# A second level of seven products for both sequence matrices, with the products of the first level in another order

## The chip, the cores and the metric

The kernel runs on one core of one Trainium2 chip. The metric is the device time of one execution in microseconds; lower is better.

## The reference

The input is x, 2048 tokens by 640 features. One branch is a Fourier mixing layer, real part only, with given cosine and sine matrices; the other is a dense layer, Mish, and a second dense layer. A gate per token mixes them.

```python
a = einsum("bsd,ed->bse", x, dft_hid_re)       # 640 x 640
b = einsum("bsd,ed->bse", x, dft_hid_im)
y = einsum("ts,bse->bte", dft_seq_re, a) - einsum("ts,bse->bte", dft_seq_im, b)   # 2048 x 2048
h = einsum("bsd,df->bsf", x, w1) + b1          # F = 1728
m = einsum("bsf,fd->bsd", h * tanh(softplus(h)), w2)
g = sigmoid((x * gate_w).sum(-1, keepdims=True))
out = g * y + (1 - g) * m
```

Everything is fp32. The kernel multiplies the sequence matrices onto x first and the hidden matrices after that.

## The kernel before

**One product.** A product of two fp32 blocks is three matmuls (`mm3`): each operand is split into a high and a low fp32r part, and high x high, high x low and low x high are summed in PSUM. A matmul has 128 x 128 weights and 512 moving columns, a whole PSUM bank. For a moving operand (`operand`) ScalarE copies the high part and VectorE subtracts it for the low part; weights are cut the same way (`split`).

**Seven for eight.** The large products are written as a scheme of seven block products in place of eight (Winograd's form). A `Problem` takes two token tiles of 512 columns (`t1`, `t2`), two halves of the contraction (k and k + `kh`) and four of the five 128-column weight groups; the fifth group is multiplied plainly. A `Stage` makes the weight sums: `top` loads three weight columns, `low` makes the sums t1 to t4 and loads the lower half (`XB`: fifth, b21, b22). The stages are `seq` (kh = 8, weights from x, moving tiles from the cosine and sine matrices), `hid` (kh = 5) and `fin` (kh = 6, weights from w2).

A `Problem` has three parts. `first` multiplies a11 b11. `second` loads a11, a21 and a22 for each k and makes three products: a22 with t4, s2 with t2, s1 with t1. `third` loads a12, and a11, a21, a22 again except for the last `HOLD` k, whose sums stay in SBUF, and makes a12 with b21 ("12"), s3 with t3, s4 with b22. The sums between are `tt`, a VectorE tensor_tensor. After each product the banks are combined with further additions.

**The second level.** `Halves` takes a12 b21 of two problems together (token tiles 0 and 2) and makes it with seven products again, with sums of its own of weights (`top`) and of moving tiles. `UNITS = (1,)` says that this is done for problem q=1 and its partner q=3, the sine matrix; q=0 and q=2, the cosine matrix, make "12" plainly in `third`. The same form is used in the last stage.

**Order.** The sequence part runs second(0), third(0), second(1), third(1), the unit, second(2), third(2), second(3), third(3). Then come the hidden problems, the first dense layer and the last stage. The program is first a graph of operations (`Graph`); matmuls keep their written order, and a planner (`Graph.run`) places the operations of ScalarE, VectorE and the two DMA issuers (SP for loads, POOL for stores) by modelled costs and wanted times (`want`, `by`, `since`), and gives out tiles from pools. The pools are 8 PSUM banks, 10 operand pairs `r`, 18 fp32 tiles `f` of 512 columns, 6 fp32 tiles `x` of 640 and 26 weight pairs `w`. A pool that nobody asks for any more passes its tiles to another (`heir`).

**Beside it.** Sixteen gate sums (L1211) are spread over 60 to 210 us by their wanted times. In the last stage the weight sums are made ahead through DRAM (`make`, from `MADE`), and `rest` multiplies the last rows of w2, five blocks for a token tile.

## Time and profile before

| | |
|---|---|
| median of 3 runs | 852.66 us (852.25 to 852.85) |
| profiled execution | 852.38 us, its span 850.6 us |
| granted TensorE clock | 0.999 of full |
| TensorE (PE) busy | 845.2 us, 99%, 3715 instructions |
| weight loads (PEld) | 697.2 us, 82% |
| VectorE (DVE) | 748.1 us, 88%, 1358 instructions |
| ScalarE (ACT) | 525.7 us, 62%, 977 instructions |
| HBM | 182.39 MB read, 55.66 MB written, 280 GB/s |

Times are of one profiled execution, counted from the span's start. A busy share is an average over all stages. Lines such as L369 are those of the helpers: L369 is every product's matmul, L333 is `tt`, L342 is `copy`, L363 and L364 are `operand`, L355 is `split` on VectorE, L324 a store and L1211 a gate sum. The program's names stand without buffer numbers: `f<-ps` is a copy from a PSUM bank into an f tile. The duration of an instruction on VectorE overlaps the start of the next.

### The profile page before, as it was taken

Reading aid. Unit: us, or ns where it says so; the run is one execution under the profiler, and the core shown is the slowest. Engines: PE = TensorE matmul, PEld = TensorE weight load, DVE = VectorE, ACT = ScalarE, POOL = GpSimd, SP = SyncE. Lnnn points to the kernel's source line nnn. Section 1 sums busy time; section 2 is a strip of 40 time slices with the busy share of each in tenths; the row PEclk is TensorE's granted clock in tenths of the full one; section 3 lists DMA queues with packets and bytes.
Section 4 is the critical chain, followed back from the end, with each engine's and each line's share of the span. In section 5 each row is a group of like instructions: output and inputs, shape, how many; then the busy total and the mean of one; then the engine's idle time right before and its main releaser. Section 6 shows DMA issues by size and latency. Waiting matters only on the chain.

```text
span 850.6 us, 12496 instructions
## 1 busy us (share of the span) xinstructions
PE 845.2 (99%) x3715; PEld 697.2 (82%) x3715; DVE 748.1 (88%) x1358; ACT 525.7 (62%) x977; POOL 115.3 (14%) x210
## 2 busy tenths in 40 slices
PE   9999999999999999999999999999999999999998
PEld 7888888888888788888888888888888888888886
DVE  7977889977789988887999999999696889999987
ACT  6967765537456646454678773666578877544623
POOL 0122110002001111040012102003431110002100
PEclk9999999999999999999999999999999999999999
DMA  9898695768567897999999875858999799849974
GB/s 332 319 357 283 191 326 156 258 228 298 173 215 248 291 383 250 329 363 384 329 332 326 263 262 195 297 186 304 383 326 336 244 321 334 264 124 269 317 267 173
DMA packets 119603, 238.90 MB, mean 281 GB/s; under 512 B 15200, under 2 KB 23136, under 8 KB 119536
## 3 DMA queue, kind: packets, MB, share of 16 engines
q1 hardware_dynamic: 102512, 184.95, 64.6%
q0 software_dynamic: 16880, 53.03, 17.7%
q8 instruction: 29, 0.48, 0.2%
q14 instruction: 38, 0.31, 0.1%
q10 hardware_dynamic: 144, 0.13, 0.0%
HBM read 182.39 MB, written 55.66 MB: 280 GB/s over the span
## 4 chain that ended last, share of the span: by engine, by line
PE 94%; DVE 3%; DMA 2%; issue 1%; ACT 0%; DVEq 0%; ACTq 0%
PE ps L369 93%; DVE f L333 2%; DMA f<-in_xn_dram 1%; PE ps L1189 0%; DMA f<-in_c_im_dram 0%; DVE r2l L364 0%; DVE r1l L364 0%; DVE ps L333 0%; DVE r8l L364 0%; DVE r3l L364 0%; DVE r4l L364 0%; DVE r9l L364 0%; DVE r7l L364 0%; DVE r6l L364 0%; ACT r2h L363 0%
## 5 line engine op out<-in xcount | busy, mean ns | idle before, releaser
L333 DVE TENSOR_TENSOR f<-f,f 128x512 f32<-128x512 f32 (+1 forms) x371 | 238.5, 662 | 17.3 <-DMA f<-late 5.9
L342 ACT ACTIVATE f<-ps 128x512 f32<-128x512 f32 x177 | 102.6, 595 | 41.3 <-PE ps L369 36.2
L333 DVE TENSOR_TENSOR f<-ps,f 128x512 f32<-128x512 f32 x100 | 65.7, 685 | 18.9 <-PE ps L369 16.8
L342 ACT ACTIVATE ps<-f 128x512 f32<-128x512 f32 x77 | 45.5, 597 | 9.2 <-DVE f L333 8.3
L324 POOL DMA_DIRECT2D act<-f x52 | 28.3, 544 | 134.9 <-ACT f L815 110.1
L324 POOL DMA_DIRECT2D u<-f x40 | 21.6, 543 | 175.9 <-DVE f L333 161.4
L815 ACT ACTIVATE f<-f,b1s 128x512 f32<-128x512 f32 x36 | 26.1, 724 | 29.7 <-DVE f L333 29.7
L363 ACT ACTIVATE r5h<-f 128x512 fp32r<-128x512 f32 x42 | 26.4, 630 | 26.0 <-DVE f L333 15.7
L363 ACT ACTIVATE r7h<-f 128x512 fp32r<-128x512 f32 x42 | 26.4, 629 | 20.0 <-PE ps L369 10.1
L363 ACT ACTIVATE r1h<-f 128x512 fp32r<-128x512 f32 x41 | 25.8, 628 | 18.9 <-DVE f L333 7.8
L363 ACT ACTIVATE r3h<-f 128x512 fp32r<-128x512 f32 x42 | 26.4, 627 | 17.2 <-PE ps L369 10.5
L333 DVE TENSOR_TENSOR x<-x,x 128x256 f32<-128x256 f32 (+3 forms) x80 | 35.6, 458 | 1.0 <-DMA x<-in_xn_dram 0.9
L363 ACT ACTIVATE r4h<-f 128x512 fp32r<-128x512 f32 x41 | 25.8, 630 | 17.0 <-PE ps L369 13.9
L363 ACT ACTIVATE r2h<-f 128x512 fp32r<-128x512 f32 x37 | 23.3, 629 | 20.9 <-DVE f L333 10.2
L363 ACT ACTIVATE r9h<-f 128x512 fp32r<-128x512 f32 x40 | 25.2, 629 | 17.0 <-PE ps L369 14.6
L363 ACT ACTIVATE r6h<-f 128x512 fp32r<-128x512 f32 x38 | 23.9, 629 | 18.9 <-PE ps L369 12.2
L363 ACT ACTIVATE r8h<-f 128x512 fp32r<-128x512 f32 x38 | 23.9, 628 | 15.9 <-PE ps L369 9.7
L363 ACT ACTIVATE r0h<-f 128x512 fp32r<-128x512 f32 x36 | 22.6, 628 | 16.4 <-PE ps L369 7.4
L364 DVE TENSOR_TENSOR r9l<-f,r9h 128x512 fp32r<-128x512 f32 x40 | 27.4, 685 | 4.2 <-ACT r9h L363 4.1
L364 DVE TENSOR_TENSOR r3l<-f,r3h 128x512 fp32r<-128x512 f32 x42 | 28.8, 685 | 2.3 <-ACT r3h L363 2.3
L364 DVE TENSOR_TENSOR r5l<-f,r5h 128x512 fp32r<-128x512 f32 x42 | 28.8, 686 | 2.2 <-ACT r5h L363 1.8
L364 DVE TENSOR_TENSOR r7l<-f,r7h 128x512 fp32r<-128x512 f32 x42 | 28.8, 686 | 2.0 <-ACT r7h L363 2.0
(2371 smaller groups left out, 2745.4 us busy)
## 6 DMA issues: line engine op xcount, KB each, us to landing
f<-in_c_im_dram SPq DMA_DIRECT2D x126, 256.0 KB, 4.5
f<-in_c_re_dram SPq DMA_DIRECT2D x110, 256.0 KB, 4.8
f<-act SPq DMA_DIRECT2D x89, 256.0 KB, 5.2
f<-u SPq DMA_DIRECT2D x62, 256.0 KB, 4.8
act<-f POOLq DMA_DIRECT2D x52, 256.0 KB, 4.9
f<-in_xt_dram SPq DMA_DIRECT2D x42, 256.0 KB, 4.9
u<-f POOLq DMA_DIRECT2D x40, 256.0 KB, 4.1
x<-in_xn_dram SPq DMA_DIRECT2D x24, 320.0 KB, 3.8
```

Of the source, the lines that this page charges most:

```text
L324: dma(queue, lambda: ISSUE[queue].dma_start(d.t, v.t[:rows]), whole(v), whole(d), rows * N * 4)
L333: dve(lambda: nc.vector.tensor_tensor(o.t[rows, x], a.t[rows, y], b.t[rows, z], op=op), whole(a, b), whole(o), n)
L342: act(lambda: nc.scalar.activation(o.t, a.t, AF.Copy, scale=scale), whole(a), whole(o))
L363: act(lambda: nc.scalar.activation(r.t[0][:, :N], src.t[:, :N], AF.Copy), whole(src), [(r, 0)])
L364: dve(lambda: nc.vector.tensor_tensor(r.t[1][:, :N], src.t[:, :N], f32(r.t[0][:, :N]), op=OP.subtract), whole(src) + [(r, 0)], [(r, 1)])
L369: G.add("PE", lambda: nc.tensor.matmul(bank.t, w.t[wn][:, k * P:k * P + P], x.t[xn_][:, :N], start, stop, skip_group_check=True), [(w, (k, ...
L815: act(lambda: nc.scalar.activation(o.t[rows], src.t[rows], AF.Mish, **more), whole(src, table) + whole(b1s) * bias, whole(o), more=0.1)
```

## The change

`UNITS` becomes (0, 1): a12 b21 of the cosine matrix is made by a second unit of seven, which stands after third(0); q=0 and q=2 no longer make "12". The sums of the unit's weights are made once, so they move from the unit of q=1 to that of q=0.

In `second` the products are now s3 with t3, s2 with t2, s1 with t1; a22 with t4 ("22") moves to `third`. s2 is kept from `second` to `third`, in SBUF in the sequence and hidden stages (`HOLD_S2`), through DRAM in the last one, so `third` loads a12 and a22 only (and s2 in the last stage). The banks' combination changes with it: the s3 product (`c22`) is added to bank `a` and to the result on VectorE, and `rest` of t2 moves from the start of `second` to its end.

The lower weights `XB` are loaded and split by `late` in `third` instead of by `low`; the loads of `low` in the sequence stage wait for 70 us. In the unit the fourth product's bank is now the copy `c1` and the sum with `u2` is made at the end. f tiles may be borrowed from the x pool (`lender`). `MADE` starts at 560 us instead of 590, and the planner's DMA rate is 364 in place of 370 KB per us.

```diff
-RATE = 370e3
+RATE = 364e3
-MADE = 590.0, 6.0
+MADE = 560.0, 6.0
+LEND = 0.0
+LOWS = {8: 70.0, 5: 0.0}
-HOLD = {8: 3, 5: 3, 6: 0, 7: 0}
-UNITS = (1,)
+HOLD = {8: 0, 5: 0, 6: 0, 7: 0}
+HOLD_S2 = {8: 8, 5: 5, 6: 0, 7: 0}
+UNITS = (0, 1)
+LATE = (8, 5)
...
+        def spare(p):
+            q = p.lender
+            return max(0, len(q.free) - bisect_left(q.asks, (now + LEND,))) if q else 0
...
+    FS.lender = X
...
+        def late(self, k):
+
+            if k in self.XB:
+                return
+            g = load(X, self.row(k + self.kh), cols=D)
+            if self.neg:
+                copy(g, g, -1.0)
+            self.XB[k] = Val(W)
+            split(self.XB[k], 0, g, 0, D)
...
-            for p, k in in_turn(kh, *[("22", "s2", "s1")] * 3):
-                if p == "22":
+            for p, k in in_turn(kh, *[("s3", "s2", "s1")] * 3):
+                if p == "s3":
                     low(k)
                     a22, a21, a11 = self.moving(t2, k + kh), self.moving(t2, k), self.moving(t1, k)
+                    tt(a21, a21, a11, OP.subtract)
...
-                        tt(a21, a21, a22, OP.add)
-                        tt(a11, a21, a11, OP.subtract)
-                        own.update({("22", k): a22, ("s1", k): a21, ("s2", k): a11})
+                        s2 = a22
+                        tt(s2, a22, a21, OP.add)
+                    if k >= kh - HOLD_S2[kh + self.last]:
+                        self.held["s2", k] = s2
+                    else:
+                        store(self.kept[k], s2)
+                    tt(a11, s2, a11, OP.add)
+                    own.update({("s3", k): a21, ("s1", k): a11, ("s2", k): s2})
...
                 elif p == "s2":
-                    u2 = [self.add_y(v, y, 2 + j, t1) for j, v in enumerate(self.a)]
+                    u2 = [to_sbuf(v) for v in self.a]
+                    for v, o in zip(self.a, c22):
+                        tt(v, v, o, OP.add)
...
+            for v, u, o in zip(b, u2, c22):
+                tt(v, v, u, OP.add)
+                tt(o, v, o, OP.add)
...
                     a12 = self.moving(t1, k + kh)
-                    if k in self.held:
-                        a21, a22 = self.held.pop(k)
-                    else:
-                        a11, a21, a22 = self.moving(t1, k), self.moving(t2, k), self.moving(t2, k + kh)
-                        tt(a21, a21, a11, OP.subtract)
-                        tt(a22, a22, a21, OP.add)
-                    tt(a22, a12, a22, OP.subtract)
-                    own.update({("12", k): a12, ("s3", k): a21, ("s4", k): a22})
+                    s2 = self.held.pop(("s2", k)) if ("s2", k) in self.held else load_of(FS, self.kept[k])
+                    tt(s2, a12, s2, OP.subtract)
+                    own.update({("12", k): a12, ("s4", k): s2})
+                if p != "s4":
+                    st.late(k)
...
-                elif p == "s3":
-                    product(self.a, st.blocks("t3", k), x, False, end)
-                    product([self.d2], st.blocks("five", k), x, False, end)
+                elif p == "22":
+                    product(self.a, st.blocks("t4", k), x, False, end)
+                    product([self.d2], st.blocks("low5", k), x, False, end)
...
                 (c, c1), d1 = self.part.c, self.part.d1
-                for o, v, q in ((c, p, c), (d1, d, d1), (u2, u2, c1)):
+                for o, v, q in ((c, p, c), (d1, d, d1), (u2, b, u2)):
                     tt(o, v, q, OP.add)
-            tt(b, b, u2, OP.add)
+                b = c1
+            if self.into:
+                tt(b, b, u2, OP.add)
...
-                for v, j in ((c, 0), (d1, 4), (b, 1)):
+                tt(u2, b, u2, OP.add)
+                self.give(1, t1, u2)
+                for v, j in ((c, 0), (d1, 4)):
                     self.done(v, j, t1)
```

## Rows read from the trace of the kernel before

**Rows 1.** The page, busy time of each engine, us, share of the span, instructions.

```profile
PE 845.2 (99%) x3715; PEld 697.2 (82%) x3715; DVE 748.1 (88%) x1358; ACT 525.7 (62%) x977; POOL 115.3 (14%) x210
```

**Rows 2.** Waits of TensorE: engine, line, releaser; us in total, times, longest.

```profile
PE ps L1189 <- PEq L1361: 0.8, 1, 0.8
PE ps L369 <- DVE ps L333: 0.5, 1, 0.5
```

**Rows 3.** The chain that ended last: start us, us, what.

```profile
285.30 561.33 PE ps L369 x2475
```

**Rows 4.** Windows by stage: length, each engine's busy us (x instructions), clock, DMA.

```profile
70.00:118.00 48.00, 48.00 (x213) 39.77 (x212) 36.85 (x77) 34.52 (x69) 9.26 (x18) 1.00 0.78 265
118.00:156.80 38.80, 38.80 (x173) 32.10 (x172) 37.89 (x79) 26.00 (x53) 1.08 (x2) 1.00 0.66 211
156.80:200.30 43.50, 43.50 (x193) 36.03 (x192) 35.77 (x63) 19.49 (x33) 4.20 (x8) 1.00 0.69 237
200.30:238.40 38.10, 38.10 (x170) 31.53 (x169) 29.36 (x48) 21.25 (x36) 1.23 (x3) 1.00 0.69 231
238.40:265.60 27.20, 27.20 (x122) 22.52 (x121) 25.73 (x52) 12.96 (x25) 1.63 (x3) 1.00 0.61 199
265.60:296.00 30.40, 29.89 (x132) 24.45 (x131) 29.99 (x56) 21.28 (x40) 3.82 (x8) 1.00 0.93 302
```

**Rows 5.** Timeline at the one wait: start us, us, engine, line, operation.

```profile
283.36 0.68 DVE L333 TENSOR_TENSOR f<-ps,f 128x512 f32<-128x512 f32 x1
...
283.96 0.68 DVE L333 TENSOR_TENSOR f<-f,f 128x512 f32<-128x512 f32 x1
...
284.56 0.69 DVE L333 TENSOR_TENSOR ps<-ps,f 128x512 f32<-128x512 f32 x1
...
285.30 0.50 PE L369 MATMUL ps<-r2h,w9h 128*128 128x512 f32 x1 [0.51 <-DVE ps L333]
```

**Rows 6.** Timeline of VectorE, narrower and wider operations.

```profile
60.58 0.76 DVE L333 TENSOR_TENSOR x<-x,x 128x256 f32<-128x256 f32 x2
...
66.89 0.82 DVE L355 TENSOR_TENSOR w11l<-x,w11h 128x640 fp32r<-128x640 f32 x1
67.63 0.68 DVE L333 TENSOR_TENSOR f<-ps,f 128x512 f32<-128x512 f32 x1
...
72.83 0.28 DVE L355 TENSOR_TENSOR w10l<-x,w10h 128x128 fp32r<-128x128 f32 x1
73.03 0.28 DVE L355 TENSOR_TENSOR w12l<-x,w12h 128x128 fp32r<-128x128 f32 x1
```

**Rows 7.** Windows by stage, weight splits of VectorE (L355) alone.

```profile
118.00:156.80 38.80, 9.56 (x20) 1.00 0.66 211
```

**Rows 8.** Timeline at the end of second(0), TensorE, then ScalarE.

```profile
153.17 0.39 PE L369 MATMUL ps<-r5h,w8l 128*128 128x512 f32 x1
...
153.85 0.39 PE L369 MATMUL ps<-r5h,w21l 128*128 128x512 f32 x1
...
156.79 0.39 PE L369 MATMUL ps<-r7h,w13h 128*128 128x512 f32 x1
...
153.61 0.58 ACT L342 ACTIVATE f<-ps 128x512 f32<-128x512 f32 x1
...
154.61 0.59 ACT L342 ACTIVATE f<-ps 128x512 f32<-128x512 f32 x1
```

**Rows 9.** Windows: the last stage's two second parts, then the busiest slice.

```profile
700.00:736.00 36.00, 36.00 (x160) 29.81 (x159) 35.26 (x66) 25.24 (x51) 1.61 (x3) 1.00 0.95 324
...
783.00:818.00 35.00, 35.00 (x156) 29.00 (x155) 31.09 (x52) 16.32 (x29) 4.25 (x6) 1.00 1.00 326
...
380.00:400.00 20.00, 20.00 (x90) 16.57 (x89) 13.86 (x23) 7.91 (x14) 2.69 (x5) 1.00 1.04 383
```

More of the change, by code (lines that the diff above doesn't have):

```diff
@@ L3 @@
 from contextlib import ExitStack
+from itertools import count
 import concourse.bass as bass
@@ L176, in granted, with take @@
             return True
+        def spare(p):
+            q = p.lender
+            return max(0, len(q.free) - bisect_left(q.asks, (now + LEND,))) if q else 0
+        def take(v):
+            p = v.pool
+            if p.free:
+                return p.free.pop(0)
+            q = p.lender
+            t = q.free.pop(0)
+            v.home = q, t
+            return q.part(t)
         def bequeath(p):
@@ L206, in run @@
                             v.pool.soon.remove(v.ask)
-                        v.t = v.pool.free.pop(0)
+                        v.t = take(v)
                         bequeath(v.pool)
@@ L434, in low @@
                 f, t = (load_of(X, v) for v in self.made[k])
-                g = load(X, self.row(k + self.kh), cols=D)
             else:
-                f, g = load(X, self.row(k)[:, P:]), load(X, self.row(k + self.kh), cols=D)
+                apart = self.kh in LATE
+                since = LOWS[self.kh]
+                f = load(X, self.row(k)[:, P:], since=since)
+                g = load(X, self.row(k + self.kh)[:, P * apart:], cols=D - P * apart, since=since)
                 if self.neg:
-                    copy(g, g, -1.0)
+                    n = D - P * apart
+                    act(lambda: nc.scalar.activation(g.t[:, :n], g.t[:, :n], AF.Copy, scale=-1.0), whole(g), whole(g), n)
                 t = Val(X)
-                self.sums(f, g, t, P)
+                self.sums(f, g, t, P - P * apart)
             self.top(k)
@@ L444, in low @@
                 self.T2[k // KD] = Val(W)
[L445 removed]
+            c = self.XT13[k] = Val(W)
             split(self.XA[k], 3, t, 2 * P, 2 * P)
@@ L449, in low @@
             split(c, 0, f)
-            split(b, 0, g, 0, D)
+            if self.kh not in LATE and k not in self.made:
+                self.XB[k] = Val(W)
+                split(self.XB[k], 0, g, 0, D)
     def in_turn(kh, begin, between, end, n=2):
@@ L455, in in_turn @@
         return order + [(p, k) for p in end for k in range(kh - n, kh)]
+    serial = count()
     class Problem:
@@ L464, in __init__ @@
             self.apart, self.bare = apart, bare
-            self.held = {}
+            self.held, self.kept = {}, [Val(t=dr.tile([P, N], F32, name=f"s2_{next(serial)}")) for k in range(st.kh)]
         def first(self, top):
@@ L531, in second @@
                     for j, xj in fifth:
-                        product([self.d2], st.blocks("low5", j), xj, False, j == kh - 1)
+                        product([self.d2], st.blocks("five", j), xj, False, j == kh - 1)
                 elif p == "s2":
@@ L538, in second @@
                     continue
-                if p == "22":
-                    self.p4 = [self.gated(v, j) if y else to_sbuf(v) for j, v in enumerate(p4)]
+                if p == "s3":
+                    c22 = [to_sbuf(v) for v in p7]
                     if y:
@@ L543, in second, with gated @@
                             tt(v, v, y(j, t1), OP.add)
[L544 to L561 removed]
+                elif p == "s2":
+                    u2 = [to_sbuf(v) for v in self.a]
+                    for v, o in zip(self.a, c22):
+                        tt(v, v, o, OP.add)
+            if self.rest:
+                e = [bank(), bank()]
+                self.rest(t2, self.a + e + [self.d2], (0, 1, 2, 3, 4), (0, 1, 4))
+            for v, u, o in zip(b, u2, c22):
+                tt(v, v, u, OP.add)
+                tt(o, v, o, OP.add)
+            if y:
+                for j, v in enumerate(b):
+                    tt(v, v, y(2 + j, t1), OP.add)
+            if self.rest:
+                for v, o in zip(e, c22):
+                    tt(o, v, o, OP.add)
+            if not self.bare:
+                self.c = [copy(bank(), v) for v in self.p1]
+            if self.aside and not self.bare:
+                if y:
+                    tt(self.d, self.d, y(4, t1), OP.add)
+                self.d1 = copy(bank(), self.d)
+            for j, o in enumerate(c22):
+                if y:
+                    tt(o, o, self.q(t2), OP.mult)
+                    tt(o, o, y(2 + j, t2), OP.add)
+                    self.finish(2 + j, t2, o)
+                else:
+                    self.give(2 + j, t2, o)
             self.b = b
[L564 to L565 removed]
+        def gated(self, b, d):
+            f = Val(FS)
             tt(f, b, self.q(self.t2), OP.mult)
@@ L619, in third @@
                     continue
[L620 to L634 removed]
+                if p == "22":
+                    for j, v in ((0, self.a[0]), (1, self.a[1]), (4, self.d2)):
+                        if self.y:
+                            self.finish(j, t2, self.gated(v, j))
+                        else:
+                            self.done(v, j, t2)
                 elif p == "12":
@@ L1288, in fnet_mish_gate @@
                           lambda d, t: load_of(FS, later.aside[min(d, 2)]), later.finish)
-            unit.done = sq[q].done
+            unit.done, unit.give = sq[q].done, sq[q].give
             for _ in unit.steps():
@@ L1320, in fnet_mish_gate @@
                   lambda d, t, v: store(extra[min(d, 2)], v))
-    unit.done = ou[0].done
+    unit.done, unit.give = ou[0].done, ou[0].give
     for _ in unit.steps():
```

81 lines of the change are left out of this document (18 added, 63 removed).

## The prediction, made before the result was known

> **What bounds the kernel now.** I read the page's busy shares first, then TensorE's waits, the chain that ended last, and the windows by stage. TensorE is busy 99% of the span with 3715 instructions [rows 1]: eight warm-up matmuls and 3707 of work, which is exactly what counting the calls of `mm` in the code gives. After its start it waited for another engine once in the whole program, 0.5 us, for a VectorE addition into PSUM [rows 2]. So nearly nothing can be gained by ending waits; the time is the number of matmuls times their pace. The pace is read from the long unbroken piece of the chain that ended last: 2475 matmuls in 561.33 us [rows 3], 0.2268 us each.
>
> The second thing to see is how close VectorE comes. The stretches of [rows 4] are the stages of the sequence part, from the matmul counts at that pace: second(0) from 118 to 156.8 us, third(0) to 200.3, second(1) to 238.4, third(1) to 265.6, the unit of seven to 296. VectorE is busy 37.89 of 38.80 us in second(0) and 29.99 of 30.40 in the unit; between them it has slack. The one wait sits in that unit: at 283.36, 283.96 and 284.56 three additions follow each other, and the matmul at 285.30 had waited 0.51 us for the last, the addition into bank `b` [rows 5].
>
> The Trainium skill (Perfetto Trace Analysis, "Identifying the Most-Contended Engine") says that a matmul's busy share is a poor measure of TensorE, that the weight loads' share should be used, and plain occupancy for the others. By it TensorE stands at 82%, VectorE at 88% [rows 1], VectorE would be the engine to relieve, and matmuls taken away would give nothing. The trace disagrees over the whole, since the matmuls keep one pace with one wait [rows 2, 3], and agrees in the two full stretches [rows 4].
>
> **Removed matmuls.** Problem q=0 and its partner q=2 each lose the plain "12" part: 8 k x 3 blocks x 3 matmuls = 72, together 144. The second `Halves` unit has 4 k x 11 blocks x 3 = 132. The other products are renamed and reordered, and `rest` keeps its five blocks, so 12 fewer matmuls, 3703 in all: 12 x 0.2268 = **-2.72 us**. That this is not done is excluded by the count.
>
> **The one wait.** In the unit, `tt(b, b, u2)` was the sixth addition in a row and the one waited for [rows 5]. After the change `b` is the bank `c1`, filled long before, and the sum with `u2` is made at the unit's end. So **-0.51 us**, and the new unit doesn't bring its like. Lower end of the gain: 0, if the first of the remaining additions (banks `c`, `d1`) becomes the late one.
>
> **VectorE's work.** Pitch from start to start: 0.60 us for 512 columns [rows 5], 0.74 for 640, 0.20 for 128, and a pair of 256 in 0.76, so 0.34 [rows 6]. Kept s2 saves one sum for each k that was not held: 5 in each of four sequence problems, 2 in each of two hidden, 6 in each of two last ones, 36, and the last problem some 2 more. The plain "12" of q=0 and q=2 loses 16 operands (one VectorE subtraction each). The new unit adds 28 operands, 16 sums and 9 closing additions, 53. The whole is about -1 instruction: no change in the total. What counts is where they fall. In the stretch second(0), third(0), new unit:
> - before, second(0) and third(0) took 37.89 + 35.77 = 73.66 us [rows 4];
> - less 5 sums and 8 operands, 13 x 0.60 = -7.8;
> - plus 53 x 0.60 = 31.8, plus the unit's tops, which move from the later unit to this one: 16 sums of 128 columns and 8 splits of 256, 3.2 + 2.7 = 5.9;
> - plus four splits of 640 that `late` moves in from before 118 us, 2.9.
>
> That is 106.5 us. TensorE needs 420 matmuls x 0.2268 = 95.3 us there. The excess is 11.2 us. What can go ahead: in second(0) there were 20 weight splits [rows 7], five for each `low`, so four of eight `low` were still unsplit at 118 us. Without their XB they cost up to 4 sums x 0.34 + 0.33 + 0.20 + 0.20 + 0.60 = 2.7 each, 10.7 for four, and VectorE was idle 48.00 - 36.85 = 11.15 us from 70 to 118 us [rows 4]. XB no longer takes eight weight pairs at that point, so pairs for the early `low` are there. So the stretch is just full: excess between 0.5 (all four ahead) and 11.2 us (none). Gate sums and the operands of coming products can move by a few us either way. I take **+1.0 us**, two waits of the size seen in [rows 2]; bounds 0 and 11.2. I lean to the low end because second(0) alone and the unit alone ran at 98% and 99% for 0.5 us of waiting. The following stretch (second(1), third(1), old unit) gets easier: 85.1 us of VectorE in 95.7 before, without the tops and with fewer operands' sums about 76.
>
> **New waits on TensorE's path.** `a` is now added to (`c22`) on VectorE before the next stage writes it. In the trace the last two matmuls into `a` start at 153.17 and 153.85, ScalarE reads the banks at 153.61 and 154.61, and the next stage starts at 156.79 [rows 8]. One addition after the second copy (155.20 + 0.69) ends at 155.9; the second bank is wanted at 157.5. So 0.9 to 1.6 us of cover, one or two queue places on VectorE; if VectorE is further behind, "22" waits, and then s4. There are eight such places; cost 0 to 8 x 0.6 = 4.8, taken as 0 outside the full stretch. The other end sums leave with what they replace: six additions per sequence problem before and after.
>
> **Transfers.** Sequence: 28 loads of 256 KB fewer, 16 + 3 more for the unit and 8 second loads for XB: even. Hidden: -2, +5. Last stage: 12 loads become 12 stores, moved from third to second on POOL's queue. In the first of these, XB's six loads leave the same stretch (0.95 share, 324 GB/s). In the second nothing leaves: 326 GB/s at full share [rows 9], plus 6 x 0.262 MB over 35 us = 45, 371 GB/s. The busiest slice ran 383 GB/s [rows 9] without TensorE waiting [rows 2], so I take 0; upper end 1.57 MB / 383 GB/s = 4.1 us. Weights of the last stage are made 30 us earlier, away from the denser part. Borrowed x tiles only let work start earlier; POOL's stores wait for no one but the reload, over 10 us later.
>
> **Sum.** -2.72 - 0.51 + 1.0 = -2.2. The profiled execution took 852.38 us (span 850.6 and 1.8 around it), 0.3 below the median 852.66 of the runs, within their 0.6 spread. From the median: **850.4 us**.
>
> **Rivals.**
> - *VectorE sets the pace* where it is full, and TensorE gives back what it saves: half of the excess, or three to five small waits. For: two stretches of [rows 4]. Against: one wait in the whole trace. VectorE's count is unchanged, so the time is, about 852.4 us. (By the rule of the Trainium skill above it would be so everywhere.)
> - *The excess is not met.* Place: the new unit after third(0). If the four `low` stay behind 118 us (eight held s2 tiles of eighteen f tiles leave less room to work ahead), TensorE waits up to 11.2 us: 852.7 - 3.2 + 11.2 = 860.7 us. It is slower than before once more than 3.2 of the 11 us are not moved, and by over 0.2% from 4.9. Against: before, with XB in the way, half of the `low` had been moved.
> - *The last stage's stores* delay its loads: 852.7 - 3.2 + 4.1 = 853.5, place 780 to 815 us. Against: [rows 9].
>
> **Chances.** The forecast 0.58, with a range of its own from 849.1 (no new wait, and 0.3 for the spread) to 850.9. VectorE sets the pace 0.22. Excess not met 0.13. Stores 0.07, split over the bound. A measurement tells some 0.2%, 1.7 us, from no change. So faster 0.58, same 0.25, slower 0.17. Range: 849.1 to 854.2, which leaves out the unmet excess and little else.
>
> **What would show it.** Right: 3703 TensorE instructions; no wait for the `b` addition; total waits of TensorE on VectorE under 1.5 us; fewer of the `low` splits after 118 us; chain still TensorE over 90%. Wrong: VectorE full from 140 to 215 us with TensorE waiting for `r` tiles or PSUM sums in the first unit, waits before each "22", or for loads near 800 us.

## The result and the profile after

The changed kernel takes 855.91 us (median of 16 runs, 853.99 to 862.55) where the kernel before takes 852.76 (16 runs beside them, 851.95 to 853.77). The ratio is 1.0043 with an interval of 1.0031 to 1.0054: 0.43% slower, and outside the predicted range. Four executions that were 10% to several times longer than the others of their kernel (one of e4, one of e16, two of the kernel before) stand in no median, spread or ratio here. The profiled execution took 855.2 us, its span 853.0 at a granted clock of 1.000; against the profile of the kernel before that is 2.4 us more of span and 0.4 more around it.

Line numbers have moved by 19 to 32: a matmul is now L388, `tt` L352, `copy` L361, `operand` L382 and L383, `split` L373 and L374, a load L333, a store L343, a gate sum L1243. The page, busy time of each engine (answers [rows 1]):

```profile
PE 843.6 (99%) x3703; PEld 695.2 (82%) x3703; DVE 746.2 (87%) x1357; ACT 533.2 (63%) x982; POOL 121.4 (14%) x222
```

The 12 matmuls are gone and VectorE has one instruction fewer, as counted. The waits of TensorE (answers [rows 2]; engine, line, releaser; us in total, times, longest):

```profile
PE ps L388 <- ACT f L361: 3.7, 2, 2.3
PE ps L1221 <- PEq L1393: 0.8, 1, 0.8
PE ps L388 <- ACT ps L361: 0.6, 1, 0.6
PE ps L388 <- DVE r0h L380: 0.2, 1, 0.2
```

The wait for the addition into `b` has gone too. In its place stand two waits for a copy from a bank into an f tile (the row's third number is the longer, 2.3 us; the other is 1.4), one of 0.6 us for a copy into a bank, and a small one at the start. The chain that ended last shows where (answers [rows 3]; start us, us, what):

```profile
147.13 4.17 DMA x<-in_xn_dram
...
171.07 6.54 DMA x<-in_xn_dram
...
178.30 0.83 DVE x L1243 x2
...
186.72 0.54 POOL u L343
...
187.50 4.69 DMA u<-f
...
192.29 0.61 ACT f L361
...
192.94 21.41 PE ps L388 x93
...
283.07 6.02 DMA u<-f
...
289.19 0.61 ACT f L361
...
289.84 274.79 PE ps L388 x1211
...
575.08 6.38 DMA y<-f
...
588.16 0.59 ACT ps L361
...
588.80 260.11 PE ps L388 x1145
```

Before, one piece of 2475 matmuls ran to the end from 285.30. Now TensorE is stopped at 190, at 288 and at 588 us. The first two are in the two units: a store of an f tile to DRAM (`u<-f`) takes 4.69 and 6.02 us to land, ScalarE's copy wants that tile, and the next matmul wants the bank that the copy empties. Behind the first of these stores the chain leads through VectorE's queue to two loads of 320 KB: a second load of XB at 147.13, and at 171.07 the load of a gate sum, which takes 6.54 us to land (the sum itself, L1243, starts at 178.30). The profile infers who released whom, so this is a hint and not yet a proof. The timeline of the first (start us, us, engine, line, operation):

```profile
190.26 0.39 PE L388 MATMUL ps<-r9h,w4l 128*128 128x512 f32 x1
...
192.29 0.60 ACT L361 ACTIVATE f<-ps 128x512 f32<-128x512 f32 x1 [1.79 <-DMA u<-f]
...
192.94 0.50 PE L388 MATMUL ps<-r5h,w4h 128*128 128x512 f32 x1 [2.30 <-ACT f L361]
```

The windows by stage, in the bounds that the stages now have (answers [rows 4]: second(0), third(0), the new unit; then 148 to 176 us by itself; the length, the busy us of TensorE, weight loads, VectorE, ScalarE and GpSimd, clock, DMA share, GB/s):

```profile
118.00:156.80 38.80, 38.80 (x173) 32.15 (x172) 37.08 (x75) 23.51 (x45) 1.20 (x3) 1.00 0.74 246
156.80:185.00 28.20, 28.20 (x126) 23.37 (x125) 27.19 (x55) 15.87 (x31) 2.47 (x5) 1.00 0.77 282
185.00:216.00 31.00, 28.70 (x127) 23.40 (x127) 30.24 (x60) 22.21 (x41) 1.88 (x4) 1.00 0.86 282
...
148.00:176.00 28.00, 28.00 (x126) 23.16 (x125) 27.32 (x50) 16.53 (x29) 1.11 (x2) 1.00 1.00 365
```

The last line against the same stretch of the kernel before:

```profile
148.00:176.00 28.00, 28.00 (x125) 23.20 (x124) 26.44 (x50) 15.21 (x29) 0.00 (x0) 1.00 0.81 270
```

VectorE is busy 94.5 of the 98 us from 118 to 216, as foreseen. What was not foreseen is the DMA: full for 28 us, 365 GB/s where it was 270. Loads land later there. The loads of the cosine matrix issued from 148 to 176 us, with the median us to landing last; after, then before:

```profile
f<-in_c_re_dram SPq DMA_DIRECT2D x16, 256.0 KB, 5.8
...
f<-in_c_re_dram SPq DMA_DIRECT2D x19, 256.0 KB, 3.9
```

ScalarE and VectorE wait for loads in this part. Their waits on transfers from 118 to 216 us, after, the longest:

```profile
ACT r5h L382 <- DMA f<-in_c_re_dram: 2.6, 1, 2.6
ACT w8h L373 <- DMA x<-in_xn_dram: 1.8, 1, 1.8
ACT f L361 <- DMA u<-f: 1.8, 1, 1.8
ACT r9h L382 <- DMA f<-in_c_re_dram: 1.8, 1, 1.8
ACT w19h L373 <- DMA x<-in_xn_dram: 1.4, 1, 1.4
```

The whole list sums to 13.5 us; the same list of the kernel before has two groups and 4.4 us. No row of the list is a gate sum that waits for its own load; it is the other loads that come late. In 148 to 176 us eight loads of `x<-in_xn_dram`, 320 KB each, are issued where there were three: the second loads of XB, by `late`, and the gate's loads meet there, and the unit's loads are beside them.

The account by starts of matmuls: -2.72 for the 12 matmuls and -0.76 for the `b` wait (0.51, and 0.25 more until the next matmuls are at pace again); +4.27 for three waits and +0.75 for their restarts; +0.3 at the start. That is +1.8 of the 2.2 us by which the last output is written later.

### The profile page after: what moved, and what is told of

It reads as the page before. It is cut to its first block, busy times and chain, and to the rows that moved or that the text cites. A ratio compares the mean times of both kernels' runs of the same rounds, so it can differ in the third digit from the quotient of the medians.

```text
span 853.0 us, 12456 instructions
## 1 busy us (share of the span) xinstructions
PE 843.6 (99%) x3703; PEld 695.2 (82%) x3703; DVE 746.2 (87%) x1357; ACT 533.2 (63%) x982; POOL 121.4 (14%) x222
## 4 chain that ended last, share of the span: by engine, by line
PE 77%; issue 10%; DMA 5%; DVE 5%; POOL 1%; ACT 1%; SPq 0%; POOLq 0%; ACTq 0%; DVEq 0%
PE ps L388 77%; DVE f L352 1%; DMA u<-f 1%; DMA x<-in_xn_dram 1%; DMA y<-f 1%; DMA f<-in_c_im_dram 1%; POOL u L343 1%; DMA f<-in_c_re_dram 1%; DVE x L1243 0%; DMA act<-f 0%; DMA f<-in_w_dram 0%; ACT f L361 0%; DVE ps L352 0%; DVE r6l L383 0%; DVE x L352 0%
## 5 line engine op out<-in xcount | busy, mean ns | idle before, releaser
L352 DVE TENSOR_TENSOR f<-f,f 128x512 f32<-128x512 f32 (+2 forms) x321 | 205.5, 657 | 9.0 <-ACT f L847 2.1
L361 ACT ACTIVATE f<-ps 128x512 f32<-128x512 f32 x150 | 87.1, 595 | 42.3 <-PE ps L388 27.9
L352 DVE TENSOR_TENSOR f<-ps,f 128x512 f32<-128x512 f32 x102 | 68.1, 686 | 25.1 <-PE ps L388 17.1
L343 POOL DMA_DIRECT2D act<-f x50 | 27.1, 542 | 111.3 <-ACT f L847 91.3
L382 ACT ACTIVATE r1h<-f 128x512 fp32r<-128x512 f32 x39 | 24.5, 629 | 27.8 <-DVE f L352 14.9
L361 ACT ACTIVATE ps<-f 128x512 f32<-128x512 f32 x65 | 37.9, 592 | 5.7 <-DVE f L352 2.8
L343 POOL DMA_DIRECT2D u<-f x33 | 17.8, 542 | 161.3 <-DVE f L352 112.0
L352 DVE TENSOR_TENSOR x<-x,x 128x256 f32<-128x256 f32 (+3 forms) x77 | 33.5, 449 | 8.1 <-DMA x<-in_xn_dram 4.6
L382 ACT ACTIVATE r7h<-f 128x512 fp32r<-128x512 f32 x41 | 25.8, 630 | 20.2 <-PE ps L388 11.7
L382 ACT ACTIVATE r5h<-f 128x512 fp32r<-128x512 f32 x37 | 23.4, 631 | 22.9 <-DVE f L352 11.2
L382 ACT ACTIVATE r6h<-f 128x512 fp32r<-128x512 f32 x43 | 27.2, 632 | 16.3 <-PE ps L388 11.9
L382 ACT ACTIVATE r4h<-f 128x512 fp32r<-128x512 f32 x39 | 24.6, 630 | 17.9 <-PE ps L388 10.2
L382 ACT ACTIVATE r3h<-f 128x512 fp32r<-128x512 f32 x42 | 26.4, 629 | 14.9 <-PE ps L388 12.0
L383 DVE TENSOR_TENSOR r7l<-f,r7h 128x512 fp32r<-128x512 f32 x41 | 28.1, 686 | 7.8 <-ACT r7h L382 7.7
L382 ACT ACTIVATE r2h<-f 128x512 fp32r<-128x512 f32 x40 | 25.2, 631 | 14.8 <-DVE f L352 7.1
L382 ACT ACTIVATE r0h<-f 128x512 fp32r<-128x512 f32 x40 | 25.2, 629 | 12.5 <-PE ps L388 6.7
L383 DVE TENSOR_TENSOR r6l<-f,r6h 128x512 fp32r<-128x512 f32 x43 | 29.5, 685 | 3.6 <-ACT r6h L382 3.6
L383 DVE TENSOR_TENSOR r3l<-f,r3h 128x512 fp32r<-128x512 f32 x42 | 28.8, 685 | 4.3 <-ACT r3h L382 4.3
L382 ACT ACTIVATE r8h<-f 128x512 fp32r<-128x512 f32 x39 | 24.6, 630 | 10.3 <-PE ps L388 5.3
L383 DVE TENSOR_TENSOR r2l<-f,r2h 128x512 fp32r<-128x512 f32 x40 | 27.4, 686 | 4.0 <-ACT r2h L382 4.0
L382 ACT ACTIVATE r9h<-f 128x512 fp32r<-128x512 f32 x34 | 21.4, 628 | 15.2 <-PE ps L388 6.3
```

The source lines that it names most:

```text
L343: dma(queue, lambda: ISSUE[queue].dma_start(d.t, v.t[:rows]), whole(v), whole(d), rows * N * 4)
L352: dve(lambda: nc.vector.tensor_tensor(o.t[rows, x], a.t[rows, y], b.t[rows, z], op=op), whole(a, b), whole(o), n)
L361: act(lambda: nc.scalar.activation(o.t, a.t, AF.Copy, scale=scale), whole(a), whole(o))
L382: act(lambda: nc.scalar.activation(r.t[0][:, :N], src.t[:, :N], AF.Copy), whole(src), [(r, 0)])
L383: dve(lambda: nc.vector.tensor_tensor(r.t[1][:, :N], src.t[:, :N], f32(r.t[0][:, :N]), op=OP.subtract), whole(src) + [(r, 0)], [(r, 1)])
```

## The experiments

The first theory was one of tiles: f tiles are scarce, the planner believes in faster stores than there are, so copies run into tiles still being stored. The rivals were VectorE's load (the gate sums fall into its full stretch), the new order by itself, and transfers that are late. All edits are to the changed kernel unless said otherwise. Each result is the median with lowest and highest, then the ratio to the kernel before with its interval.

**e1: the planner is told that stores land later.**

```diff
-        op = G.add(queue, emit, r, w, DELAY + size / RATE, ...)
+        late = 1.2 if queue == "POOL" else 0.0
+        op = G.add(queue, emit, r, w, DELAY + late + size / RATE, ...)
...
```

> Edit: the planner is told that a transfer issued by POOL lands 1.2 us later than it assumed (about 4.1 us instead of 2.9 for 256 KB); nothing of the computation changes. Tile theory: TensorE's two waits in the units (2.3 and 1.4 us, each plus some 0.25 us of restart) come from a ScalarE copy whose only free f tile was still being stored to u. With the true landing time those copies get tiles that are free, both waits go, the time falls to about 850 us (849.5 to 851.5) and its spread narrows to that of the kernel before. VectorE theory: the copies are late because VectorE is full from second(0) to the unit; planning the stores otherwise leaves the waits, 854 to 857 us. Transfer theory: the queues are denser than before and the waits only move to loads, 853 to 857 us.

859.88 us (856.22 to 862.68), 1.0074 (1.0054 to 1.0095). Both waits for stores went, and a longer one came before them, at the first "22". The timeline of e1, VectorE and then TensorE (L354 is `tt`, L376 `split` and L390 the matmul in this kernel):

```profile
151.43 0.69 DVE L354 TENSOR_TENSOR f<-f,f 128x512 f32<-128x512 f32 x1 [1.25 <-DMA f<-in_c_re_dram]
...
156.60 0.83 DVE L376 TENSOR_TENSOR w23l<-x,w23h 128x640 fp32r<-128x640 f32 x1
...
159.15 1.89 DVE L354 TENSOR_TENSOR ps<-ps,f 128x512 f32<-128x512 f32 x3
...
159.90 0.50 PE L390 MATMUL ps<-r0h,w5h 128*128 128x512 f32 x1 [3.23 <-DVE ps L354]
```

VectorE waits 1.25 us for a load, does three weight splits of 640 columns behind it, and reaches the addition into bank `a` three microseconds late. So f tiles under store were the place of the waits in the changed kernel; with those gone the lateness shows up at another place.

**e2: fewer s2 held**, which leaves more f tiles free and costs loads.

```diff
-HOLD_S2 = {8: 8, 5: 5, 6: 0, 7: 0}
+HOLD_S2 = {8: 2, 5: 5, 6: 0, 7: 0}
```

> Edit: in the sequence stage only two of the eight s2 of a problem are held in f tiles, six go through DRAM (24 stores and 24 loads of 256 KB more). Tile theory: six of eighteen f tiles are given back between second and third, so no copy meets a tile that is being stored; waits in the units gone, about 850 us (849.5 to 852). VectorE theory: VectorE's work is the same, the waits stay, 854 to 857 us. Transfer theory: 48 transfers more in the sequence stage make it worse than the changed kernel, over 857 us.

860.95 (858.8 to 863.31), 1.0085 (1.0067 to 1.0104). Waits of 2.6 us at the "22" and 4.8 in the units; the waits on transfers of the two engines rose to 18.1 us. More free tiles with more loads is worse, as the transfer theory had it.

**e3: no gate sums.** Each sum becomes a copy of one column, the loads stay; the gate isn't computed.

```diff
-                x.t, x.t, 1.0, wide.t, op0=OP.mult, op1=OP.mult, accum_out=gcol.t[:, k:k + 1]),
+            dve(lambda k=k, x=x: nc.vector.tensor_copy(gcol.t[:, k:k + 1], x.t[:, :1]),
```

> Edit: the sixteen gate sums (L1243, 0.82 us each) are replaced by one-column copies, so the gate is not computed; their loads stay. It takes about 12 us of VectorE's work out of 50 to 205 us. VectorE theory: the excess of second(0), third(0) and the unit is gone, the wait in the first unit goes, and about 851 to 852.5 us are measured (the wait in the second unit, behind the gate sums, may stay). Tile theory: the waits for tiles under store stay, at least the second one, 853.5 to 857 us.

856.24 (854.76 to 858.75), 1.0038 (1.0025 to 1.0051). The windows of e3 from 118 to 216 us:

```profile
118.00:216.00 98.00, 96.28 (x424) 79.16 (x423) 90.80 (x181) 63.95 (x119) 6.00 (x11) 1.00 0.79 269
```

VectorE falls from 94.51 to 90.80 of the 98 us, and TensorE still stands there for 1.7 us. The waits of VectorE and ScalarE on transfers are 7.8 us, 3.4 of them of the one-column copies for their own loads. Nothing is won.

**e4: the new order without the new unit.**

```diff
-UNITS = (0, 1)
+UNITS = (1,)
```

> Edit: all of the change except the second unit: UNITS stays (1,), so q=0 and q=2 make 12 plainly, with 3707 matmuls of work. It tells what the new order, the kept s2, the late XB and the lent tiles do by themselves. Tile theory: the eight held s2 and the stores are there too, so waits of the same kind can appear in the one unit: 852 to 856 us. VectorE theory: without the second unit the stretch is not full, so no new waits: 852 to 853 us, as before.

857.05 (855.47 to 857.48), 1.0039 (1.0028 to 1.0051), longer than either expectation. The stretch from 118 to 216 us is free of TensorE waits; the DMA share in 148 to 176 is 0.81. Its one wait of note is of 2.75 us at 588, where the first dense layer begins, with some 3 us of half the clock at its end (see the last section). So the order by itself costs nothing in the sequence part, and the loss of e4 is that of the last stage's weights, which e7 takes up.

**e5: the gate's sums and their loads earlier**, over 40 to 115 us in place of 60 to 210.

```diff
-GATES = 60.0, 10.0
+GATES = 40.0, 5.0
```

> Edit: the wanted times of the sixteen gate sums move from 60 to 210 us to 40 to 115 us (GATES 40, 5), so that nothing of the computation changes and about 7 us of VectorE's work leaves the stretch from 118 to 213 us. VectorE theory (as it stands after the first four runs: VectorE's queue is full from second(0) on, so any load that lands late shifts everything behind it, and TensorE waits at the places with least cover): lateness shrinks, the waits of the first unit get shorter or go, the second one (behind 210 us) is helped less: 852 to 855 us. Tile theory: the copies still meet tiles under store; waits at both units as in the changed kernel, 855 to 857 us.

849.96 (849.44 to 851.01), 0.9962 (0.9949 to 0.9974), faster than either expectation. The waits of VectorE and ScalarE on transfers are 1.7 us, the DMA share in 148 to 176 us is 0.82, and both unit waits are gone. VectorE is as full as ever, 95.60 of 98 us.

**e6: e5 and e1 together.**

```diff
-GATES = 60.0, 10.0
+GATES = 40.0, 5.0
...
+        late = 1.2 if queue == "POOL" else 0.0
...
```

> Edit: gate sums early as in the run before, and the planner told that stores land 1.2 us later, as in the first run. The landing edit alone took both waits of the units away and got a wait of 3.2 us for an addition into bank a at the end of second(0), where VectorE was behind. If both causes are needed together (full VectorE and tiles under store), neither the units' waits nor the one at 156 us should be there, and only some 0.5 to 1 us at 588 us remains: 850 to 852.5 us. If the store edit is bad by itself, the time stays at 857 to 861 us.

850.65 (849.57 to 852.72), 0.9969 (0.9959 to 0.998). Later stores in the plan add nothing.

**e7: the last stage's weights made later.**

```diff
-MADE = 560.0, 6.0
+MADE = 575.0, 6.0
```

> Edit: MADE starts at 575 us instead of 560 (590 in the kernel before); nothing else. It tests the third place, at 588 us, where in the changed kernel a copy into PSUM for the first dense stage came 0.6 us late behind stores of the hidden stage's y and of the last stage's weight sums. If these stores are the cause, the wait at 588 us goes and 0.5 to 1.5 us are won: 854 to 855.5 us. If it isn't, no change: 855 to 857 us, with the wait in place.

854.48 (851.98 to 857.94), 1.0017 (1.0002 to 1.0031). The wait at 588 is gone, those in the units remain (1.6 and 0.9 us), and 1.2 us stand at the "22". In the changed kernel the stores `wf` and `wt` of `make` stand among those of `y` from 560 to 590 us, and land in 6.3 and 7.0 us. None of the three plans with 575 (e7, e11, e15) waits there; of the fifteen profiles of the changed kernel and its variants with 560, twelve do, for 0.3 to 2.8 us.

**e8: the unit alone**, the kernel before with one edit.

```diff
-UNITS = (1,)
+UNITS = (0, 1)
```

> Edit: the kernel before with UNITS = (0, 1) and nothing else of the change: the same 3703 TensorE instructions with the old order, the old holding of sums and no lent tiles. VectorE theory: here 36 more sums are made, so the stretch is fuller than in the changed kernel and waits are longer: 857 to 865 us. Tile theory: without eight held s2 there is room, 851 to 855 us.

867.63 (867.05 to 868.4), 1.0168 (1.0152 to 1.0184). TensorE waits 6.2 us near 114 us for a weight split behind a load, and 2.9 and less in other places. Without the other parts the unit costs 14 us, more than either expectation; they are needed, but not enough.

**e9: the sums without the gate's loads** (on other data, so the gate isn't computed).

```diff
-            x = load(X, tokens[k], cols=D, since=GATES[0] - 20 + k * GATES[1])
-                x.t, x.t, 1.0, wide.t, op0=OP.mult, ...
+                wide.t, wide.t, 1.0, wide.t, op0=OP.mult, ...
...
```

> Edit: the sixteen gate loads of 320 KB and their x tiles are left out; the sums are made at the same times, of the gate weights with themselves, so the gate is wrong and VectorE's work is the same. Load theory (formed on the runs so far: the sums' loads and x tiles between 118 and 213 us delay the loads of XB and of the moving tiles; moving them away won 3 us of waits while taking the sums alone away won nothing): waits at the end of second(0) and in both units go, 849.5 to 851.5 us. VectorE theory: the sums still fill VectorE, so the waits stay, 854 to 857 us.

852.64 (850.78 to 855.08), 0.9997 (0.9985 to 1.001). All the sums are there, and 0.4% is won over e3, which had all the loads. VectorE and ScalarE wait for no transfer at all from 118 to 216 us. The time lies between the two expectations: in the profile short waits are left, the longest of 0.7 us in the first unit.

**e10: loads of 16 columns and no sums** (the gate isn't computed).

```diff
-            x = load(X, tokens[k], cols=D, ...)
+            x = load(X, tokens[k][:, :16], cols=16, ...)
...
```

> Edit: as the run without gate sums, but each gate load brings 16 columns instead of 640, at the same times and into an x tile as before. Beside that run (856.2 us) only the bytes are gone, 5.2 MB; the x tiles and the number of transfers stay. If the bytes are what delays the other loads: 849.5 to 852 us, without waits in the units. If it is the taking of x tiles (which are then not lent to sums, and not free for XB): 854 to 857 us.

851.27 (850.56 to 856.53), 0.999 (0.9976 to 1.0004). DMA share 0.77 in 148 to 176; waits on transfers of 6.3 us, 4.6 of them of the one-column copies for the small gate loads. Beside e3 only the bytes of these loads are gone, and 0.5% is won.

**e11: e5 and e7 together.**

```diff
-GATES = 60.0, 10.0
+GATES = 40.0, 5.0
...
-MADE = 560.0, 6.0
+MADE = 575.0, 6.0
```

> Edit: the changed kernel with the gate sums early (GATES 40, 5) and MADE at 575 us. The first removed every wait but the one at 585 us (1.4 us and restart), the second removed that one in its own run. Both together, if the places are independent: 849.96 less 1.6, so 848 to 849.5 us, faster than both kernels, with no wait of TensorE after its start. If the earlier weight sums only move the wait into the first dense stage: 849.5 to 851 us.

849.6 (848.08 to 850.95), 0.9959 (0.9943 to 0.9974): the lowest median, not told apart from e5. Its profile has no wait near 588 and one of 1.4 us at 351, for a `tt` on VectorE.

**e12: two tiles of their own for the unit's copies**, one operand pair fewer.

```diff
-NR, NFS, NX, NW = 10, 18, 6, 26
+NR, NFS, NX, NW = 9, 18, 6, 26
-            p, d = to_sbuf(a), to_sbuf(d1)
+            p, d = (copy(Val(FS if self.into else OWN), v) for v in (a, d1))
...
```

> Edit: the two first copies of a sequence unit get f-sized tiles of their own, in which no store runs; the space comes from one operand pair (NR 9 instead of 10). Gate sums and MADE as in the changed kernel. Tile theory: both unit waits (3.7 us and restarts) go, 851 to 853 us, more if nothing else is late. Load theory: copies and operands are late since loads are late, and one operand pair fewer makes it worse: 855 to 860 us, waits at other places of the same stretch.

859.86 (858.47 to 863.2), 1.0086 (1.0065 to 1.0106). As in e1, the copies no longer wait and the addition at 158 us does, 2.9 us. This is the second time that the theory of tiles falls, though with one operand pair fewer the run is not a clean one.

**e13: the gate's loads on POOL's queue.**

```diff
-            x = load(X, tokens[k], cols=D, since=...)
+            x = load(X, tokens[k], cols=D, queue="POOL", since=...)
```

> Edit: the sixteen gate loads are issued by POOL instead of SP, at the same wanted times, into the same x tiles, with the same sums. Queue theory (in SP's queue a gate load that waits for its x tile holds up the loads behind it): waits of the stretch go, 850 to 852 us. Byte theory (the other loads land late since 5.2 MB more pass in the stretch): the waits stay, 854 to 857 us.

860.67 (857.27 to 864.71), 1.0088 (1.0065 to 1.0112). SP's queue is relieved and the time is longer than both expectations: the waits on transfers are 16.5 us. A gate load holding up those behind it in SP's queue is thus no sufficient cause; but on POOL's queue the same loads stand among the stores, which may cost something of its own.

**e14: copies from DRAM to DRAM in the place of the gate's loads**, of the same bytes, issued by SP; the sums as in e9 (the gate isn't computed).

```diff
+            o = Val(t=dr.tile([P, D], F32, name=f"gs{k}"))
+            dma("SP", lambda k=k, o=o: nc.sync.dma_start(o.t, tokens[k]), [], whole(o), P * D * 4)
...
```

> Edit: as the run without gate loads (852.6 us; the gate is not computed), and at the same times SP issues sixteen copies of 320 KB from DRAM to DRAM in their place: the queue places and the bytes are back (each byte is also written to DRAM), the x tiles are not taken. Byte theory: back to 854.5 to 858 us. Queue theory, in its form that the x tile is what a gate load waits for: these copies wait for nothing, so 851.5 to 853.5 us as without loads.

853.12 (851.19 to 855.52), 1.0001 (0.9989 to 1.0012). The windows of e14 from 148 to 176 us:

```profile
148.00:176.00 28.00, 28.00 (x125) 23.17 (x125) 27.26 (x51) 16.97 (x29) 1.11 (x2) 1.00 0.97 338
```

A share of 0.97 and 338 GB/s beside a VectorE that is busy 27.26 of 28 us, and yet TensorE doesn't wait from 118 to 216 us, the waits on transfers are 3.9 us, and the time is as good as e9's. So a high share beside a full VectorE isn't the whole of the cause.

**e15: e11, with stores planned 1.5 us later.**

```diff
-GATES = 60.0, 10.0
+GATES = 40.0, 5.0
...
-MADE = 560.0, 6.0
+MADE = 575.0, 6.0
...
+        late = 1.5 if queue == "POOL" else 0.0
...
```

> Edit: the changed kernel with GATES 40, 5, MADE 575 and the planner told that stores land 1.5 us later. The best version so far had 849.6 us and one wait of 1.4 us. If late stores are what is left: no wait over 0.5 us and 848 to 849.5 us. If the rest is loads that land late: waits of about a microsecond somewhere else and 849.5 to 851.5 us.

850.65 (849.31 to 851.07), 0.9967 (0.9955 to 0.9979). As in e6, no better than without.

**e16: the changed kernel again**, without an edit.

> The changed kernel itself, unedited, on the chip of these runs, for comparison: 854 to 858 us, and waits of a copy in the two units as before in its profile, of 1 to 3 us, since they hang on how late a store or a load lands.

856.48 (853.39 to 860.12), 1.0042 (1.0028 to 1.0056): the result repeats. In its profile TensorE also waits at the "22", 1.0 us in two waits.

**e17: no borrowed x tiles.**

```diff
-    FS.lender = X
```

> Edit: the changed kernel without lending (FS.lender is not set), so x tiles serve loads, gate sums and weight sums alone; gate sums and MADE as in the changed kernel. x tile theory: between 118 and 216 us VectorE and ScalarE wait less for transfers than the 13 to 14 us of the changed kernel (under 8), and the unit waits shrink. New waits before 118 us are to be expected, where sums then find no f tile, some 3 us, so the time itself can stay at 854 to 858 us. If x tiles are not the link: the waits for transfers between 118 and 216 us stay at 10 us or more.

863.93 (859.47 to 866.46), 1.0121 (1.01 to 1.0142). TensorE waits at ten places between 67 and 598 us, and VectorE and ScalarE wait 8.9 us on transfers from 118 to 216 us, between the two values that the expectation named. It tells only that borrowing is worth some 7 us (1.0121 against 1.0043), not what it does to the gate's loads: inconclusive.

**e18: e5 again**, without a further edit.

> The run with the gate sums early (GATES 40, 5), unedited, again: 849.5 to 851 us, 0.3 to 0.45% faster than the kernel before, no wait of TensorE between 118 and 300 us of over 0.5 us.

849.98 (848.78 to 850.81), 0.9968 (0.9956 to 0.998). The waits of TensorE in e18, complete:

```profile
PE ps L1221 <- PEq L1393: 0.8, 1, 0.8
```

Its chain that ended last (start us, us, what):

```profile
4.48 838.33 PE ps L388 x3695
```

And its windows over the first three stages, and from 148 to 176 us:

```profile
118.00:216.00 98.00, 98.00 (x435) 81.15 (x434) 97.05 (x190) 65.86 (x123) 7.39 (x14) 1.00 0.77 259
148.00:176.00 28.00, 28.00 (x125) 23.21 (x124) 28.00 (x52) 16.36 (x30) 1.11 (x2) 1.00 0.86 288
```

All 3695 matmuls of work are one piece of the chain, at 0.2269 us each. This is the fastest of the five executions, 1.2 us below their median; the profile of e5, the same program, has one wait of 1.4 us at 583. VectorE has 28.00 of 28.00 us in the stretch in which the changed kernel fell behind, and TensorE never waits.

## Why the prediction was wrong

**Removed matmuls and the one wait: right.** 3703 instructions, no wait for `b`. In e18's profile, with nothing new in the way, the span is 846.9 against 850.6: -3.7, of which the 12 matmuls are 2.72 and the wait with its restart 0.76. (The medians of e5 and e18 are 3.3 and 2.5 us below those of the kernel before.) The Trainium skill (Perfetto Trace Analysis, "Identifying the Most-Contended Engine") would name VectorE, at 88% against 82% of weight loads, the most contended engine; for TensorE it also puts the share of the peak arithmetic rate beside the weight loads, which the prediction left out. In e18 TensorE set the time alone, with VectorE busy 97.05 of 98 us in the fullest stretch.

**VectorE's work: right in place, wrong on the way and in what it costs.** The stretch is full (94.5 of 98 us; 97.05 in e18), and taken as +1.0 it cost nothing in e18. The sign that was to tell it, fewer splits after 118 us, didn't come. Weight splits in second(0), after (answers [rows 7]):

```profile
118.00:156.80 38.80, 8.34 (x19) 1.00 0.74 246
```

Three of the nineteen are splits of XB, 640 columns wide, which `late` brings into this window; four of the twenty before were. So `low` has sixteen splits there before and after (and in e18), and none of it went ahead. By the sum that leaves 106.5 us of work where 94.5 were done. Counted by starts from 118 to 216 us, the sums and splits of weights are there as foreseen (16, 12 and 8), but of the 512-column operations there are 62 operand subtractions and 48 of `tt`, where the counts before (47 and 41 in second(0) and third(0)), changed as the sum says, come to 67 and 61: 18 x 0.60 = 10.8 us too much. That the stretch came out just full, as foreseen, is luck: two errors that cancel.

The rival "The excess is not met" had the sign and the place, and its condition holds, since the four `low` stay behind 118 us. But e18 meets the same condition without a wait, so it is not what made the kernel slower. The rival "VectorE sets the pace" had the full stretch, but e3 takes VectorE's load away and wins nothing, while e18 has more of it and wins everything.

**New waits: one place right, one missing.** The two longest waits of the profiled execution, 2.30 and 1.38 us for a copy out of a bank in the two units, stand at places for which the prediction has no cost; a TensorE that waits in the first unit is only among its signs of being wrong. The "22" it does name: [rows 8] gave the "22" 0.9 to 1.6 us of cover. It holds in the profiled execution and fails where VectorE is late: 0.8 us in e16, 2.6 in e2 and e13, 2.9 in e12, 3.2 in e1.

**Transfers: the step that failed.** The sum has no term for transfers in the sequence part. "Sequence: 28 loads of 256 KB fewer, 16 + 3 more for the unit and 8 second loads for XB: even" was counted over the whole sequence part, while VectorE's work two paragraphs above was laid out by stretch. The loads that left were seven in each of the four problems; of those that came, XB's eight and the unit's stand from some 148 us on, in a part (118 to 216 us) into which nine of the sixteen gate loads fall. What stands in the place of that nothing is lateness: in the profiled execution the waits in the two units cost 3.7 us and their restarts 0.5, against 3.5 won. The windows from 118 to 216 us, before, after and in e14:

```profile
118.00:216.00 98.00, 98.00 (x434) 81.12 (x433) 86.32 (x162) 54.99 (x100) 6.51 (x12) 1.00 0.71 239
...
118.00:216.00 98.00, 95.70 (x423) 78.92 (x422) 94.51 (x188) 61.58 (x115) 5.55 (x11) 1.00 0.79 268
...
118.00:216.00 98.00, 98.00 (x434) 81.00 (x433) 95.02 (x186) 64.73 (x119) 6.52 (x12) 1.00 0.79 267
```

So the stretch carries 12% more than before, and within it 28 us went from 270 to 365 GB/s, where VectorE has no slack to make up for a late load. A count by stretch would have warned of this; it would not have priced it, for e14 moves as much beside as full a VectorE, and TensorE has no wait there. [Rows 9] had shown 326 GB/s at a share of 1.00, and 383, without a wait, and they were taken as a reason for a cost of 0. In these two VectorE was busy 31.09 of 35 and 13.86 of 20 us; but the third line there, 0.95 and 324 GB/s beside 35.26 of 36 us, had no wait either. The share of the DMA and of VectorE do not tell which stretch fails. What tells it is whether the loads came in time.

That the gate's loads are the part that matters rests on the grouping of the plans, since each edit also shuffles the written order and so moves single waits. The four plans with gates at 40 and 5 (e5, e6, e11, e15; e18 repeats e5) have ratios from 0.9959 to 0.9969. The three without full gate loads (e9, e10, e14) have 0.999 to 1.0001. The seven others that have both the unit and the gates at 60 and 10 (e1, e2, e3, e7, e12, e13, e17) have 1.0017 to 1.0121, and the changed kernel itself 1.0043. The ratios of the groups don't overlap (the intervals of e7, and of e6, e15 and e18, overlap those of the middle group), and they follow the loads and not the sums: with both 1.0043, without the sums 1.0038 (e3), without the loads 0.9997 (e9), without the sums and nearly all bytes of the loads 0.9990 (e10). The time that VectorE and ScalarE wait on transfers from 118 to 216 us sets the slow group apart as well: 7.8 to 18.1 us in the profiles of the changed kernel and of the seven others, 0 to 6.3 in the three without full loads, 1.7 to 3.1 in the five early ones.

**Last stage: wrong in a second, smaller way.** "Weights of the last stage are made 30 us earlier, away from the denser part": they now meet the stores of `y`. That is the wait at 588 us, 0.59 us in the changed kernel's profile and 2.75 in e4; e7, e11 and e15 are without it. By the medians e7 wins 0.26% over the changed kernel, with intervals that just touch; beside early gates (e11 against e5) nothing is left to win. The rival of the last stage's stores, near 800 us, did not occur: the chain runs unbroken from 588.80 on.

**Open.** What it is in a gate load that does the harm isn't settled. Its bytes alone are not it (e14), its place in SP's queue alone seems not to be (e13), the x tile alone isn't (e10, where the load is small). SP waited about as long in total in all of these from 118 to 216 us (64.5 us after, 68.7 before, 67.8 in e18; 61 to 71 in e9, e10, e13 and e14). That an x tile is held through a long load, and is then missing as a tile to borrow, would agree with all three; it is argued, not shown, since e17 changed too much to tell. Nor is it shown how the wait in the second unit, at 288 us and far behind the last gate sum (200.8 us), hangs on these loads: the plans with early gates and e9 are rid of it or nearly so (0 to 0.6 us), e10 and e14 keep 1.3 and 0.9 us.

The best versions are e5 and e11: 0.9962 (0.9949 to 0.9974) and 0.9959 (0.9943 to 0.9974) of the kernel before, some 3 us faster than it and 7 faster than the changed kernel, e5 by two numbers of the plan and e11 by three.

## What to carry to other kernels

Lay the transfers of a change out by stretch, as the engines' work, and not as a total: an even count can still put all that is new in one place. An engine that works through its queue in order can be full without harm as long as its inputs come in time (VectorE 28.00 of 28.00 us in e18, no wait of TensorE). Full and late together are not harmless, because nothing makes up for a late load, and the wait shows up far from it, wherever the cover is least (a load issued at 171 us, a wait at 190). Shares and GB/s don't tell the two cases apart here; the time that the engines wait on transfers does. So when work is added to a full stretch, look first for side work with its loads that may stand elsewhere.

## What the runs showed of the hardware

After some waits of TensorE the granted clock was half for a while. Windows of e16 around the wait at 194 us (length, PE busy and matmuls, granted clock, DMA share, GB/s):

```profile
180.00:190.00 10.00, 10.00 (x46) 1.00 0.56 178
191.72:194.60 2.88, 1.01 (x4) 0.98 0.90 336
194.60:197.60 3.00, 3.00 (x9) 0.50 1.03 381
198.00:208.00 10.00, 10.00 (x46) 1.00 0.83 258
```

TensorE stood 1.87 us, started two matmuls at full clock, and was then granted 0.50, the 1.2 GHz level, for some 3 us: eight matmuls that start 0.43 us apart, 1.6 us lost. The same followed waits of 2.75 us (e4) and 2.19 (e13), but neither the 2.30 of the changed kernel's profile nor the 3.23 of e1. With it a wait can cost nearly twice its length. The changed kernel's runs spread over 8.6 us where those of before spread over 1.8; the longest of them (861.03 and 862.55) have mean clocks of 0.995 and 0.996, the profiled one 1.000, which agrees with such stretches, though those runs have no profile.

A recorded clock of 0.95, on the other hand, went with no loss: it stands throughout the profiled execution of e9, and its long piece, 369.06 us for 1626 matmuls, still goes at 0.2270 us each. Whether the clock itself was lower or only its record isn't known.

The stores of 256 KB into `u` landed in 4.1 us before and 5.3 after (median), where the planner counts 2.9.
